# A logit copy on ScalarE, a reordered last block and later gathers in a fused attention-and-routing kernel

## The chip, the cores and the metric

The kernel runs on one core of one Trainium2 chip. The time is the device time of one execution in microseconds; where a run was repeated, the median is given. Everything else comes from a hardware profile of one execution, whose times are counted from the start of its span.

The engines of the core are PE (TensorE, matrix products; it takes transposes too), DVE (VectorE), ACT (ScalarE), POOL (GpSimd, which here also issues the gathers and scatters by row number) and SP (SyncE, which issues plain loads). Each runs its own list of instructions in order and waits on semaphores of the others. [...] DVE and ACT bring results from PSUM to SBUF.

## What is computed

Banded attention with a few global keys, then a mixture of experts in which each token goes to one expert:

```python
B, H, S, D = 4, 8, 768, 64            # n_global 8, n_local 96
scores = scale * q @ k.T  - slope[h] * dist     # only keys j < 8, or 0 <= i - j < 96
a   = exp(scores - max); a /= sum(a) + 1e-9
att = a @ v                            # (B, H, S, D), float32
x   = att.transpose(0, 2, 1, 3).reshape(B * S, H * D)     # 3072 tokens x 512

logits = x @ w_gate                    # 8 experts
e      = argmax(logits); gate = softmax(logits)[e]
out[t] = gate[t] * relu(x[t] @ w1[e]) @ w2[e]             # w1 512 x 1024, w2 1024 x 512
```

## The kernel before

The attention part goes over 24 blocks of 128 query tokens (4 sequences of 6 blocks). A block n needs its own 128 keys and the block before it, into whose first 32 rows the global keys and values of the sequence have been mixed. The blocks are software-pipelined: turn n of the loop computes the scores of block n, transposes q and k of block n+1, turns block n-2 into token rows, and multiplies the exponentials of block n-1 with their values.

```python
ps_s = tile_pool("ps_s", bufs=2, PSUM)     # scores, two banks each
ps_t = tile_pool("ps_t", bufs=3, PSUM)     # transposes, values, token rows
ps_r = tile_pool("ps_r", bufs=1, PSUM)     # row sums and logits: ONE buffer

def transposed(ps, dst, src, on, scale=1.0):
    pt = ps.tile([P, NPAIR, P], F32, tag="t", name="pt")
    for m in range(NPAIR):
        nc.tensor.transpose(pt[:, m, :], ..., ident[:])
    if on == "act":
        nc.scalar.activation(dst, pt[:], AF.Copy, bias=0.0, scale=scale)
    else:
        nc.vector.tensor_copy(out=dst, in_=pt[:])
# prep_q(n): transposed(..., "act", QS);  prep_k(n): transposed(..., "act" if n else "dve"),
# and POOL then makes ka, the keys of block n with the global keys in their first 32 columns

def mix_v(n):                              # global values into the block before
    if n % NBLK > 1:
        nc.gpsimd.tensor_copy(out=vts[n - 1][0:GW], in_=vts[n - n % NBLK][0:GW])

# scores(n): 16 to 32 matmuls into two sp tiles, DVE adds the bias: p <- sp, other
# exps(n, groups): ACT, p <- exp(p), one instruction of 128x1024 for each of two groups
# both(n): DVE, pb <- p[own keys] + p[keys before], two instructions of 128x512

def values(n):
    for m in range(NPAIR):                 # po tiles, two m in each
        ... nc.tensor.matmul(po[...], lhsT=vt[...], rhs=ps[n][...])
        if m % 2:
            nc.scalar.copy(ots[n][:, m - 1:m + 1], po[:, 0:2])
    pr = prs[n] = ps_r.tile([P, 4, P], F32, tag="r", name="pr")
    all_p = pbs.pop(n, None) or [p[:, :, :, 1, :] for p in ps[n]]
    ... nc.tensor.matmul(pr[..., 0, :], lhsT=one_in, rhs=all_p[...])      # row sums
    ... nc.tensor.matmul(pr[..., 0, :], lhsT=gate_w, rhs=ots[n][...])     # logits
    nc.scalar.copy(rs[:], pr[:, 0, :])
    return rs

def tokens(n, rs):
    nc.tensor.transpose(pr[:, 1, :], rs[:], ident[:])     # into the same pr bank
    ... nc.tensor.transpose(px[:, m, :], ot[:, m, :], ident[:])           # x4
    part = pr[:, 1, :].rearrange("p (m c) -> p m c", c=GW)
    nc.vector.tensor_scalar(den, part[...], 1e-9, None, ALU.add)
    nc.vector.reciprocal(rden, den)
    nc.vector.tensor_tensor(lh, part[...], rden, ALU.mult)
    nc.vector.tensor_reduce(lg[:, i, :], lh, AX.X, ALU.add)
    nc.vector.tensor_tensor(xr[...], px[...], rden, ALU.mult)
    # after the last block of a sequence: choose() = five small DVE instructions

for n in range(N + 1):                     # N = 24
    if n < N: scores(n)
    if n + 1 < N: prep_q(n + 1)
    ...
    if 0 < n <= N: both(n - 1)
    if n + 1 < N: prep_k(n + 1)
    if n < N and n != 1: exps(n, slice(0, 1 if n else 2))
    ...
    if n >= 2: tokens(n - 2, rs.pop(n - 2))            # and gates() for a whole sequence
    if n: rs[n - 1] = values(n - 1)
    if 0 < n < N: exps(n, slice(n != 1, 2))
    if n == N: ex.x_in_s(0, ps_t.tile(...))
    if n < N: mix_v(n)
    if i == 2 and b == B - 1:              # b, i = divmod(n - 2, 6): this is turn 22
        send()                             # two scatters of token rows to DRAM
        ex.early()
    ...                                    # dispatch() of a sequence: slots for its tokens
tokens(N - 1, rs.pop(N - 1))
```

`early` computes row numbers with eight small DVE instructions (the fifth gives `grow_s`), and has POOL gather two tiles of 128 finished token rows from DRAM (`xs <- xs_dram, grow_s`). `x_in_s` transposes such a tile on PE (`pt <- ident, xs`) and DVE copies it to SBUF (`xsT <- pt`). With it the first product of the experts begins (`up_s`, `u <- xsT, w`), about 163 us into the span; the experts fill the rest.

Of the kernel before, what the change touches and what calls it, by code (L numbers as in the profile page):

```python
# [9 lines left out]
F32 = mybir.dt.float32  # L10
BF16 = mybir.dt.bfloat16
I32 = mybir.dt.int32
AF = mybir.ActivationFunctionType
# [10 lines left out]
def kernel(  # L24
# [12 lines left out]
    nc = tc.nc  # L37

    P = 128
    B, H, S, D = q.shape  # L40
# [4 lines left out]
    NPAIR = H // 2  # L45
    NDC = DM // P
    NFC = F // P
    GW = 32
# [181 lines left out]
        nc.vector.tensor_tensor(x.rearrange("p (h d) -> p h d", d=D), po[:],  # L230
                                den[:].unsqueeze(2).to_broadcast([P, H, D]), ALU.mult)

    def transposed(ps, dst, src, on, scale=1.0):

        pt = ps.tile([P, NPAIR, P], F32, tag="t", name="pt")
        for m in range(NPAIR):
            nc.tensor.transpose(pt[:, m, :], src[:, 2 * m:2 * m + 2, :].rearrange("p a d -> p (a d)"),  # L237
                                ident[:])
        if on == "act":
            nc.scalar.activation(dst, pt[:], AF.Copy, bias=0.0, scale=scale)  # L240
        else:
            nc.vector.tensor_copy(out=dst, in_=pt[:])  # L242

    QS = 1.0 / float(D) ** 0.5

# [4 lines left out]
    def banded(stack, rt, pool, rows, ex, den_all):  # L250
# [29 lines left out]

        def prep_q(n):
            qts[n] = raw.tile([P, NPAIR, P], F32, tag="qt", bufs=2, name="qt")
            transposed(ps_t, qts[n][:], rawt[n]["q"], "act", QS)

        def prep_k(n):
            b, i = divmod(n, NBLK)
            kind = dict(tag="kt0") if i == 0 else dict(tag="kt", bufs=3)
            kts[n] = seq.tile([P, NPAIR, P], F32, name="kt", **kind)
            transposed(ps_t, kts[n][:], rawt[n]["k"], "act" if n else "dve")
            if i == 0:  # L290
                kas[n + 1] = kts[n][:]
            elif i + 1 < NBLK:
                t = raw.tile([P, NPAIR, P], F32, tag="ka", bufs=2, name="ka")
                nc.gpsimd.tensor_copy(out=t[:, :, GW:P], in_=kts[n][:, :, GW:P])  # L294
                nc.gpsimd.tensor_copy(out=t[:, :, 0:GW], in_=kts[n - i][:, :, 0:GW])
                kas[n + 1] = t[:]
# [78 lines left out]
        def exps(n, groups):  # L375
            for p in ps[n][groups]:
                z = p[:].rearrange("p a j t c -> p (a j) t c")
                z = z[:, :, 1, :] if n % NBLK == 0 else p[:].rearrange("p a j t c -> p (a j t c)")
                nc.scalar.activation(z, z, AF.Exp)  # L379
# [12 lines left out]
        def values(n):  # L392
            vals = [(t, vts[n - 1 + t]) for t in range(n % NBLK == 0, 2)]
            ots[n] = work.tile([P, NPAIR, P], F32, tag="ot", name="ot")
            for m in range(NPAIR):
                if m % 2 == 0:
                    po = ps_t.tile([P, NPAIR, P], F32, tag="t", name="po")
                for x, (t, vt) in enumerate(vals):
                    for a in range(2):
                        nc.tensor.matmul(po[D * a:D * a + D, m % 2, :], lhsT=vt[:, 2 * m + a, :],  # L400
                                         rhs=ps[n][m // 2][:, a, m % 2, t, :], start=(x == 0),
                                         stop=(x == len(vals) - 1), skip_group_check=True)
                if m % 2:
                    nc.scalar.copy(ots[n][:, m - 1:m + 1], po[:, 0:2])

            pr = prs[n] = ps_r.tile([P, 4, P], F32, tag="r", name="pr")
            all_p = pbs.pop(n, None) or [p[:, :, :, 1, :] for p in ps[n]]
            for a in range(2):
                for m in range(NPAIR):
                    nc.tensor.matmul(pr[GW * m:GW * m + GW, 0, :], lhsT=one_in[:, a, :],  # L410
                                     rhs=all_p[m // 2][:, a, m % 2, :], start=(a == 0),
                                     stop=False, skip_group_check=True)
            for m in range(NPAIR):
                nc.tensor.matmul(pr[GW * m:GW * m + GW, 0, :], lhsT=gate_w[:, m, :], rhs=ots[n][:, m, :],
                                 start=False, stop=True, skip_group_check=True)
            rs = work.tile([P, P], F32, tag="rs", name="rs")
            nc.scalar.copy(rs[:], pr[:, 0, :])
            del ps[n]
            return rs

        def tokens(n, rs):

            b, i = divmod(n, NBLK)
            pr, ot = prs.pop(n), ots.pop(n)
            nc.tensor.transpose(pr[:, 1, :], rs[:], ident[:])
            px = ps_t.tile([P, NPAIR, P], F32, tag="t", name="px")
            for m in range(NPAIR):
                nc.tensor.transpose(px[:, m, :], ot[:, m, :], ident[:])
            if i == 0:
                seqs[b] = new_rows(rows)  # L430
            xr, lg = seqs[b]
            part = pr[:, 1, :].rearrange("p (m c) -> p m c", c=GW)
            den, rden = den_all[:, 0, n, :], den_all[:, 1, n, :]
            nc.vector.tensor_scalar(den.rearrange("p (m a) -> p m a", a=2), part[:, :, 2 * E:2 * E + 2],
                                    1e-9, None, ALU.add)
            nc.vector.reciprocal(rden, den)
            shape = [P, NPAIR, 2, E]
            lh = work.tile(shape, F32, tag="lh", name="lh")
            nc.vector.tensor_tensor(lh[:], part[:, :, 0:2 * E].rearrange("p m (a e) -> p m a e", e=E),
                                    rden.rearrange("p (m a) -> p m a", a=2).unsqueeze(3)  # L440
                                    .to_broadcast(shape), ALU.mult)
            nc.vector.tensor_reduce(lg[:, i, :], lh[:].rearrange("p m a e -> p e (m a)"), AX.X, ALU.add)

            def x_rows():
                nc.vector.tensor_tensor(xr[:, i, 0:DM].rearrange("p (h d) -> p h d", d=D),
                                        px[:].rearrange("p m (a d) -> p (m a) d", d=D),
                                        rden.unsqueeze(2).to_broadcast([P, H, D]), ALU.mult)

            if n < N - 1:
                x_rows()  # L450
                if i == NBLK - 1:
                    seqs[b] += choose(pool, rt, xr, lg)
            else:
                seqs[b] += choose(pool, rt, xr, lg)
                x_rows()
# [9 lines left out]
        def send():  # L465
            for _ in range(min(2, len(sends))):
                sends.pop(0)()

        rs = {}
        for n in range(N + 1):  # L470
            if n < N:
                scores(n)
            if n + 1 < N:
                prep_q(n + 1)
            if n == 2:
                numbers = ex.clear_s()
            if n == 3:
                ex.numbers(*numbers)
            if n in (3, 4):
                biases(0, range(4 * n - 12, 4 * n - 8), "pool")  # L480
            if 0 < n <= N:
                both(n - 1)
            if n + 1 < N:
                prep_k(n + 1)
            if n < N and n != 1:
                exps(n, slice(0, 1 if n else 2))
            if n == 0:
                biases(1, (0, 1, 2, 3), "act")
            if n == 0:
                spare = ps_r.tile([P, 512], F32, tag="r", name="spare")  # L490
                for _ in range(4):
                    nc.tensor.matmul(spare[:], lhsT=idle[:, 0:P], rhs=idle[:], start=True, stop=True)
            if n + 3 < N:
                load(n + 3)
            for load_ in feed.pop(n, ()):
                load_()

            if n - 2 < N - NBLK + 2:
                send()
            b, i = divmod(n - 2, NBLK)  # L500
            if n >= 2:
                tokens(n - 2, rs.pop(n - 2))
                if i == 0 and b:
                    xr, _, oh, gates = seqs[b - 1]
                    gates()
            if n:
                rs[n - 1] = values(n - 1)
            if 0 < n < N:
                exps(n, slice(n != 1, 2))
            if n == N:  # L510
                ex.x_in_s(0, ps_t.tile([P, NPAIR, P], F32, tag="t", name="pt"))
            if n < N:
                mix_v(n)
            if i == 2 and b == B - 1:
                send()
                ex.early()
            if i == 0 and b > 0:
                sends += dispatch(pool, ps_t.tile([P, 512], F32, tag="t", name="pr"), rt, xr, oh)
                if b == B - 1:
                    send()  # L520
# [807 lines left out]
```

## Time and profile before

| what | value |
|---|---|
| time, median of 3 runs | 521.27 us (519.11 to 521.93) |
| span of the profiled execution | 514.3 us |
| 5 to 150 us (the blocks): PE busy | 140.7 us of 145 |
| the same: DVE, ACT, POOL busy | 115.9, 88.6, 51.7 us |
| 150 to 165 us (end of the blocks): PE busy | 12.2 us of 15, at a mean granted clock of 0.89 |
| 165 to 300 us (experts): PE busy | 134.5 us of 135 |
| 300 to 500 us (experts): PE busy | 199.2 us of 200 |

The rows by stretch are the sums of the view of busy time by window. "Busy" counts an engine's instructions; what an engine waits for is in the view of waits, where each line names the waiting instruction, the one that released it, the total in us, the number of times and the longest wait. In the timeline each line has the start and the length in us, the engine, the line of the kernel and the operation, with the number of instructions merged; a bracket at its end is the idle time before it and what ended that. The granted clock of PE is a share of full speed.

### The profile page before, as it was taken

What the parts mean: (1) busy time and instruction counts of PE and PEld (TensorE: products, weight loads), DVE (VectorE), ACT (ScalarE), POOL (GpSimd) and SP (SyncE); (2) the same over time, 40 slices, a digit from 0 to 9 for tenths busy, and PEclk for the clock granted to TensorE, in tenths of its full rate; (3) what the DMA queues carried; (4) which work ended last, traced back from release to release, by engine and by line L of the source; (5) the groups of instructions that cost most, each with busy time, mean ns of one, the idle gap of its engine ahead of it and who ended that gap; (6) DMA issues with size and microseconds to landing.
All of it is one profiled execution on the core that took longest, in us unless ns stands there. A gap on an engine that the chain in (4) does not pass through costs nothing.

```text
span 514.3 us, 12403 instructions
## 1 busy us (share of the span) xinstructions
PE 498.3 (97%) x5019; PEld 423.2 (82%) x5019; DVE 313.2 (61%) x665; ACT 159.4 (31%) x321; POOL 189.4 (37%) x285
## 2 busy tenths in 40 slices
PE   8999999999998999999999999999999999999995
PEld 5888888888887679679799688869969868896984
DVE  4777877977885747529588078128527705822741
ACT  4656666665652002112112012113102212211120
POOL 5531261251442574334373074034316305502503
PEclk9999999999998999999999999999999999999998
DMA  9998789799921331074191470047254108400101
GB/s 185 212 226 222 166 242 228 173 234 222 317 91 43 124 95 43 8 253 173 42 390 33 164 261 25 1 159 275 79 214 166 26 1 280 163 2 24 43 4 50
DMA packets 96333, 72.76 MB, mean 141 GB/s; under 512 B 79324, under 2 KB 79326, under 8 KB 96228
## 3 DMA queue, kind: packets, MB, share of 16 engines
q1 hardware_dynamic: 87808, 52.44, 37.4%
q0 software_dynamic: 7872, 19.01, 10.8%
q8 instruction: 54, 0.88, 0.7%
q14 instruction: 51, 0.42, 0.3%
q10 hardware_dynamic: 548, 0.02, 0.1%
HBM read 61.46 MB, written 14.73 MB: 148 GB/s over the span
## 4 chain that ended last, share of the span: by engine, by line
PE 82%; DVE 10%; issue 6%; POOL 1%; POOLq 0%; DVEq 0%
PE u L970 18%; PE u L798 10%; PE d L1032 9%; PE d L1041 7%; PE u L808 7%; PE sp L358 6%; PE po L400 5%; DVE p L372 4%; PE pt L237 3%; DVE pb L388 3%; PE d L808 3%; PE u L1139 3%; PE u L1114 3%; PE pr L410 2%; PE t L950 2%
## 5 line engine op out<-in xcount | busy, mean ns | idle before, releaser
L1048 DVE TENSOR_TENSOR UV<-UV,d 128x512 f32<-128x512 f32 x8 | 5.5, 688 | 110.9 <-ACT yu L1142 81.3
L732 POOL DMA_INDIRECT out_dram<-ys,to_u x8 | 8.3, 1039 | 142.6 <-ACT yu L1142 87.6
L372 DVE TENSOR_TENSOR p<-sp,other 128x1024 f32<-128x1024 f32 x40 | 47.1, 1219 | 21.4 <-PE sp L358 19.5
L798 PEld LDWEIGHTS u<-xsT,w 128*128 128x128 f32 x448 | 50.9, 192 | 2.2 <-DVE c L940 1.2
L798 PE MATMUL u<-xsT,w 128*128 128x128 f32 x448 | 51.8, 276 | 0.2 <-DVE xsT L790 0.2
L970 PE MATMUL u<-cx,c 128*128 128x128 f32 x384 | 48.1, 275 | 0.0
L379 ACT ACTIVATE p<-p 128x1024 f32<-128x1024 f32 (+1 forms) x48 | 47.3, 988 | 1.4 <-DVE p L372 1.1
L400 PE MATMUL po<-p,vt 128*64 128x128 f32 x704 | 45.1, 281 | 1.4 <-POOL vt L279 1.4
L970 PEld LDWEIGHTS u<-cx,c 128*128 128x128 f32 x384 | 45.5, 192 | 0.0
L400 PEld LDWEIGHTS po<-p,vt 128*64 128x64 f32 x704 | 39.3, 140 | 5.5 <-issue 2.7
L970 PE MATMUL u<-xT,w 128*128 128x128 f32 x256 | 39.5, 277 | 0.0
L358 PE MATMUL sp<-qt,kt 64*128 64x128 f32 x448 | 37.9, 275 | 0.9 <-DVE kt L242 0.9
L808 PE MATMUL u<-w,huT 128*128 128x512 f32 x80 | 35.1, 592 | 0.0
L970 PEld LDWEIGHTS u<-xT,w 128*128 128x128 f32 x256 | 34.2, 192 | 0.9 <-DVE cx L963 0.2
L358 PEld LDWEIGHTS sp<-qt,kt 64*128 64x128 f32 x448 | 31.0, 188 | 2.8 <-issue 2.3
L1032 PE MATMUL d<-c,ch 128*128 128x256 f32 x128 | 32.9, 379 | 0.0
L215 POOL DMA_INDIRECT xs_dram<-xr,slot_i x24 | 23.8, 993 | 17.9 <-DVE cnt L860 9.9
L294 POOL COPY ka<-kt 128x384 f32<-128x384 f32 x16 | 9.2, 576 | 56.2 <-ACT kt L240 56.2
L808 PEld LDWEIGHTS u<-w,huT 128*128 128x128 f32 x80 | 15.2, 190 | 17.0 <-issue 16.7
L388 DVE TENSOR_TENSOR pb<-p 128x512 f32<-128x512 f32 x40 | 27.9, 736 | 0.9 <-ACT p L379 0.9
L997 ACT COPY uv<-u 128x256 f32<-128x256 f32 x32 | 11.9, 373 | 51.2 <-PE u L970 51.1
L1032 PEld LDWEIGHTS d<-c,ch 128*128 128x128 f32 x128 | 24.3, 190 | 3.3
(255 smaller groups left out, 1030.5 us busy)
## 6 DMA issues: line engine op xcount, KB each, us to landing
w<-in_moe_w_dram SPq DMA_DIRECT2D x24, 1024.0 KB, 7.1
w<-in_moe_w_dram SPq DMA_DIRECT2D x16, 512.0 KB, 6.2
raw_q<-in_q_dram SPq DMA_DIRECT2D x24, 256.0 KB, 4.5
raw_k<-in_k_dram SPq DMA_DIRECT2D x24, 256.0 KB, 5.2
vt<-in_v_dram SPq DMA_DIRECT2D x24, 256.0 KB, 5.4
xs_dram<-xr,slot_i POOLq DMA_INDIRECT x24, 5.6
xg<-xs_dram,grow POOLq DMA_INDIRECT x16, 6.3
mu<-xs_dram,grow_e POOLq DMA_INDIRECT x16, 2.8
```

The source lines that it names most:

```text
L215: d = nc.gpsimd.indirect_dma_start(out=xs_dram[:], out_offset=bass.IndirectOffsetOnAxis(ap=slot_i[:, u:u + 1], axis=0), in_=xr[:, u, :].bi ...
L237: nc.tensor.transpose(pt[:, m, :], src[:, 2 * m:2 * m + 2, :].rearrange("p a d -> p (a d)"), ident[:])
L358: nc.tensor.matmul(sp[:, a, j, t, :], lhsT=kt[r, m, :], rhs=qts[n][r, m, :], start=True, stop=True, skip_group_check=True)
L372: nc.vector.tensor_tensor(z, sc, bi, ALU.add)
L379: nc.scalar.activation(z, z, AF.Exp)
L388: nc.vector.tensor_tensor(t[:].rearrange("p a j c -> p (a j) c"), z[:, :, 0, :], z[:, :, 1, :], ALU.add)
L400: nc.tensor.matmul(po[D * a:D * a + D, m % 2, :], lhsT=vt[:, 2 * m + a, :], rhs=ps[n][m // 2][:, a, m % 2, t, :], start=(x == 0), stop=(x ...
L798: nc.tensor.matmul(ph[:, i, :], lhsT=self.w[e % 2][0][:, c, ts(half * HF + i, P)], rhs=xT[:, c, :], start=(c == 0), stop=(c == NDC - 1), s ...
L808: nc.tensor.matmul(py[:].rearrange("p a b -> p (a b)"), lhsT=h[:, f, :], rhs=self.w[e % 2][1][:, f, :], start=(f == 0), stop=(f == NFC - 1 ...
L970: nc.tensor.matmul(bank[:, r, :], lhsT=lhs(k), rhs=rhs(k), start=first, stop=True, skip_group_check=True)
L1032: nc.tensor.matmul(self.half(i, j), lhsT=lhs, rhs=rhs, start=(f == 0 and j == 0), stop=True, skip_group_check=True)
L1041: nc.tensor.matmul(self.half(i, j), lhsT=lhs(f), rhs=rhs(f), start=False, stop=True, skip_group_check=True)
```

## The change

It has four parts. ScalarE copies the transposed logits and row sums of a block from the PSUM bank `pr` to SBUF, and VectorE reads the copy; the bank is then free for the next block after that copy and not after VectorE's reads. The gathers of the early rows are issued one turn later, behind the last mixing of values on POOL, so that they do not stand ahead of it in POOL's list. In the last turn the values of block 23 are computed ahead of the token rows of block 22, for which both exponentials of block 23 come together and its `pr` lies in a buffer of the scores pool. And the first transposed q and k are copied in halves, so that the first scores can start after half of each.

```diff
-    def transposed(ps, dst, src, on, scale=1.0):
+    def transposed(ps, dst, src, on, scale=1.0, parts=1):
...
-        if on == "act":
-            nc.scalar.activation(dst, pt[:], AF.Copy, bias=0.0, scale=scale)
-        else:
-            nc.vector.tensor_copy(out=dst, in_=pt[:])
+        for r in range(parts):
+            m = ts(r, NPAIR // parts)
+            if on == "act":
+                nc.scalar.activation(dst[:, m], pt[:, m], AF.Copy, bias=0.0, scale=scale)
+            else:
+                nc.vector.tensor_copy(out=dst[:, m], in_=pt[:, m])
... (prep_q and prep_k pass parts=1 if n else 2)
-            pr = prs[n] = ps_r.tile([P, 4, P], F32, tag="r", name="pr")
+            pr = prs[n] = (ps_r.tile([P, 4, P], F32, tag="r", name="pr") if n < N - 1 else
+                           ps_s.tile([P, 2, 2, 2, P], F32, tag="s", name="pr")[:, 0, 0])
... (tokens)
-            part = pr[:, 1, :].rearrange("p (m c) -> p m c", c=GW)
+            part = work.tile([P, P], F32, tag="part", name="part")
+            nc.scalar.copy(part[:], pr[:, 1, :])
+            part = part[:].rearrange("p (m c) -> p m c", c=GW)
... (loop)
-                exps(n, slice(0, 1 if n else 2))
+                exps(n, slice(0, 1 if 0 < n < N - 1 else 2))
...
+            if n == N:
+                rs[n - 1] = values(n - 1)
             if n >= 2:
                 tokens(n - 2, rs.pop(n - 2))
...
-            if n:
+            if 0 < n < N:
                 rs[n - 1] = values(n - 1)
-            if 0 < n < N:
+            if 0 < n < N - 1:
                 exps(n, slice(n != 1, 2))
...
             if i == 2 and b == B - 1:
                 send()
+            if i == 3 and b == B - 1:
                 ex.early()
```

More of the change, by code (lines that the diff above doesn't have):

```diff
@@ L282, in prep_q @@
             qts[n] = raw.tile([P, NPAIR, P], F32, tag="qt", bufs=2, name="qt")
-            transposed(ps_t, qts[n][:], rawt[n]["q"], "act", QS)
+            transposed(ps_t, qts[n][:], rawt[n]["q"], "act", QS, parts=1 if n else 2)
         def prep_k(n):
@@ L288, in prep_k @@
             kts[n] = seq.tile([P, NPAIR, P], F32, name="kt", **kind)
-            transposed(ps_t, kts[n][:], rawt[n]["k"], "act" if n else "dve")
+            transposed(ps_t, kts[n][:], rawt[n]["k"], "act" if n else "dve", parts=1 if n else 2)
             if i == 0:
```

## The prediction

> **What bounds the kernel now.** I read the page's busy shares first: PE has work for 97% of the span, so only its 16 us of idle, and any time at which its clock is lowered, can be won. The waits of PE say who holds it up:
>
> ```profile
> PE pr L410 <- DVE lh L439: 4.3, 9, 1.1
> PE po L400 <- POOL vt L279: 1.4, 1, 1.4
> PE sp L358 <- DVE kt L242: 0.9, 1, 0.9
> PE pr L425 <- ACT rs L417: 0.4, 1, 0.4
> PE u L798 <- DVE xsT L790: 0.2, 1, 0.2
> ```
>
> The change aims at the first three. Line 1 is the single `pr` bank: block n's row sums wait until VectorE has read block n-2's logits (`lh`). The timeline of PE places its nine waits: 21.5 us (0.27), 28.88 (1.06), 59.27 (0.27), 66.18 (0.33), 96.57 (0.27), 103.60 (0.45), 134.00 (0.27), 141.09 (0.52), 153.70 (0.83). The end of the blocks:
>
> ```profile
> 153.70 0.64 PE L410 MATMUL pr<-pb,one_in 128*32 128x128 f32 x16 [0.83 <-DVE lh L439]
> 155.00 0.33 PE L425 MATMUL pr<-ident,rs 128*128 128x128 f32 x1 [0.43 <-ACT rs L417]
> 157.15 3.31 PE L400 MATMUL po<-p,vt 128*64 128x128 f32 x32 [1.39 <-POOL vt L279]
> 161.27 0.66 PE L789 MATMUL pt<-ident,xs 128*128 128x128 f32 x4
> 162.71 0.49 PE L798 MATMUL u<-xsT,w 128*128 128x128 f32 x2 [0.18 <-DVE xsT L790]
> ```
>
> The values of block 23 (third line) take 3.31 us; in every full block before it the same 32 records take 1.97. The windows show why (after the stretch: length, busy time and count of PE, PEld, DVE, ACT, POOL, then the clock):
>
> ```profile
> 157.00:159.00 2.00, 1.85 (x18) 1.86 (x20) 1.06 (x3) 0.00 (x0) 1.00 (x2) 0.50 0.27 103
> 159.00:160.00 1.00, 1.00 (x14) 1.00 (x12) 0.00 (x0) 0.37 (x1) 0.00 (x0) 0.53 0.00 0
> ```
>
> With 0.76 in 156 to 157, PE ran at half clock from about 156.5 to 159.9, 3.4 us, of which 2.8 after 157.15: that cost 1.4 us beside the waits. On POOL two gathers (from 153.24 and 154.60) stood ahead of the mixing at 155.94, though its input had been free since the values of block 22 ended at 152.87.
>
> [...] the issues list has 3.7 us to landing for these two gathers, so a gather issued later is not free.
>
> **Part 1, the copy on ScalarE.** It adds 23 executed copies of 128x128; the like copy `rs` takes 0.27 us, with the next instruction 0.16 after its start. ScalarE has room (88.6 us busy of 145). What counts is the place in its list: after the first exponential of the turn, ahead of the two `ot` copies. VectorE's `den` now waits for it. In most turns that costs VectorE 0.3 us, which it has. Not in the turns that begin a sequence (7, 13, 19):
>
> ```profile
> 51.02 0.59 ACT L240 ACTIVATE kt<-pt 128x512 f32<-128x512 f32 x1
> 51.49 1.06 ACT L379 ACTIVATE p<-p 128x1024 f32<-128x1024 f32 x1
> 52.44 0.65 ACT L404 COPY ot<-po 128x256 f32<-128x256 f32 x2
> ```
>
> Here `den` started at 51.27. The copy can start at 52.44 and end at 52.71, so `den` starts at 52.77, 1.5 us late, and with it the choice of experts, which ended at 53.90 and now ends at 55.4. VectorE had 0.80 us of idle before its next large addition:
>
> ```profile
> 54.69 2.35 DVE L372 TENSOR_TENSOR p<-sp,other 128x1024 f32<-128x1024 f32 x2 [0.80 <-PE sp L358]
> 61.60 2.35 DVE L372 TENSOR_TENSOR p<-sp,other 128x1024 f32<-128x1024 f32 x2
> 63.87 1.59 DVE L388 TENSOR_TENSOR pb<-p 128x512 f32<-128x512 f32 x2
> ```
>
> The addition thus starts at 55.4, 0.7 late, and from there VectorE has no idle until 66.9; the chain that ended last runs through it there. The `pb` of block 7 ends at 58.56 + 0.72 = 59.28, that of block 8 at 65.46 + 0.72 = 66.18. PE no longer waits for `lh` (66.03) but still needs `pb`: it starts at 66.2 to 66.3, where it started at 66.18. The wait is exchanged, not removed. So the six waits at 59, 66, 97, 104, 134 and 141 us (2.1 us) give nearly nothing: 0.3 in all[...]. The `ot` copies of these three turns come 0.16 us later, which the same wait swallows.
>
> The two early waits do go. At 21.50 `pb` is ready at 20.78 and PE free at 21.19: 0.31 earlier, less 0.07 because row sums without a wait take that much longer to hand over (35.15 to 36.01 against 21.50 to 22.29), so 0.24. At 28.88 VectorE is held by extra work of that turn; `pb` ends at 28.16, PE starts at 28.27: 0.61. Part 1: 0.24 + 0.61 + 0.3 = 1.15 us.
>
> **Part 2, halves.** First scores start when half of `kt` is there, about 0.3 us earlier than 7.71. But VectorE's bias chain, which ends at 9.67, sets block 0's additions, and the scores of block 1 (10.79) need the first of those (about 10.6). I count 0.07.
>
> **Parts 3 and 4, the end of the blocks,** in times of the trace before. Both exponentials of block 23 now run ahead of the logit copy: 150.6 to 152.76, the copy to 152.93, so the row sums of block 22 start at 153.0, not 153.70, and end at 153.9. POOL mixes from 152.95 to 153.6 (0.60, as in other blocks). Values of block 23: 153.9 to 155.87 at full clock. VectorE then holds PE: `den` to `xr` of block 21 (1.55 us) from 153.0 to 154.5, `early` (1.42, from its place at 148.04 to 149.46) to 155.87, and only then the two `pb` of block 23, to 157.15. PE waits some 1.2 us, ends row sums at 157.95 and the transposes of block 22 at 158.6. The gathers wait for `grow_s` (155.3), start at 155.6 and land 3.3 later (in the raw records the first started at 153.24 and landed at 156.55): 158.9. PE transposes `xs` at 159.0; VectorE, after `xr` of block 22 (to 160.1), copies `xsT` to 160.75. First product of the experts at 160.8, where it was 162.71: 1.9 us, of which 1.4 is the lost half clock. After that nothing changes: PE is busy for 134.5 of 135 us from 165, and each engine's list is the same.
>
> Sum against the profile: 1.15 + 0.07 + 1.9 = 3.1 us, if PE keeps full clock.
>
> **Will it?** Between 155.87 and 160.8 PE has only 0.86 us of row sums, transposes and 2.2 us of idle: a low stretch of 4.9 us, where the one before (152.87 to 157.15) had 4.3. [...] A dip in the new place would fall on dense matmuls and cost up to 1.7 us. The timed runs of before may mostly have had no dip; then the end gives 0.5 us only and the sum is 1.7. Weighing no dip on either side, one before only and one after only (1.7, 3.1, near 0.2), I take 2.1: 521.27 - 2.1 = 519.2.
>
> **Rivals.** (a) All nine waits for `lh` vanish and the end runs smoothly: 4.3 + 1.4 + 1.4 + 0.4 = 7.5 us, 513.8. Against it is VectorE's unbroken run from 54.69 to 66.9. (b) The logit copy makes VectorE the bound at every sequence change and PE loses there, 0.3 us in each of three, while the gathers land late: no gain, 521 to 522. For it: at 51.27 `den` was ready 1.2 us before ScalarE can copy. (c) The gathers become the wait: were landing 5.6 us, as for the scatters in the issues list, PE would stand until 161.3 and the end would give nothing but the lost clock. The 3.3 of the same gathers speaks against it.
>
> **Range and chances.** Three runs of before spread over 2.8 us, which is as much as the gain; the sum itself runs from 0.2 (dip after only) to some 5. So 516.5 to 521.5. A gain of 2% is 10.4 us, more than all PE waits named above; a loss of 2% would need a new wait of 0.4 us in every block. Within 2%: 0.97.
>
> **What would show it.** Right: waits of PE for `lh` gone, and in their place waits for `pb` at the second and third blocks of sequences 2 to 4; VectorE's idle between turns 7 and 9 gone; `den` after the ScalarE copy at about 52.8; the gathers starting 2 us later than before; about 1 us of PE wait for `pb` ahead of the last row sums; first product of the experts some 3 us earlier than 162.71. Wrong: if the waits near 59 and 66 us vanish without a successor, part 1 is worth 2 us more; if the clock dips again between 156 and 163, the end is worth 1.5 us less; if PE waits for the gathers by more than 0.5 us, part 3 has turned into a new wait.

## The result, and the profile after

Before takes 521.16 us (median of six), after 517.15 us (median of six): a ratio of 0.993, with a 95% interval of 0.9907 to 0.9952. The change is 4.0 us faster, less than 1%. The prediction was 519.2 us, a gain of 2.1, with 516.5 to 521.5 as its range.

The profiles say something else. The profile of before is of an execution of 516.22 us, shorter than every timed run of before (519.11 to 521.93). The profile of after is of one of 517.69 us, like its timed runs (516.20 to 517.69). Laid side by side, the two profiles show after as the slower one. The waits of PE in the profile of after (us in total, times, longest):

```profile
PE pr L413 <- ACT part L436: 2.7, 4, 1.7
...
PE pr L413 <- DVE pb L390: 1.1, 3, 0.5
PE u L806 <- DVE gates L801: 0.9, 1, 0.9
...
PE pt L797 <- DMA xs<-xs_dram,grow_s: 0.7, 1, 0.7
PE sp L360 <- DVE kt L244: 0.6, 1, 0.6
```

All waits for `lh` are gone, and so is the one for the mixed values. In their place stand waits for the new copy (`part`), for the sums `pb`, for the gathers and for VectorE ahead of the experts. The timeline of PE at the end of the blocks:

```profile
155.84 0.72 PE L413 MATMUL pr<-pb,one_in 128*32 128x128 f32 x14 [1.68 <-ACT part L436]
...
156.82 1.97 PE L402 MATMUL po<-p,vt 128*64 128x128 f32 x32
159.26 0.41 PE L413 MATMUL pr<-pb,one_in 128*32 128x128 f32 x4 [0.47 <-DVE pb L390]
...
162.06 0.63 PE L797 MATMUL pt<-ident,xs 128*128 128x128 f32 x4 [0.65 <-DMA xs<-xs_dram,grow_s]
...
164.15 3.81 PE L806 MATMUL u<-xsT,w 128*128 128x128 f32 x32 [0.91 <-DVE gates L801]
```

The values of block 23 take 1.97 us, at full clock (they took 3.31), but the first product of the experts starts at 164.15, where before had 162.71. The stretches that showed the half clock before (length, busy time and count of PE, PEld, DVE, ACT, POOL, then the clock):

```profile
157.00:159.00 2.00, 1.79 (x32) 1.54 (x30) 1.90 (x10) 0.74 (x3) 0.53 (x1) 1.00 0.00 0
159.00:160.00 1.00, 0.55 (x9) 0.28 (x13) 0.81 (x2) 0.21 (x1) 0.70 (x2) 1.00 0.00 0
```

And the turn that begins the second sequence, on ScalarE and VectorE, as the prediction looked at it:

```profile
50.76 1.06 ACT L381 ACTIVATE p<-p 128x1024 f32<-128x1024 f32 x1
51.71 0.27 ACT L436 COPY part<-pr 128x128 f32<-128x128 f32 x1
...
52.01 0.17 DVE L439 TENSOR_SCALAR den_all<-part 128x8 f32<-128x8 f32 x1 [1.40 <-ACT part L436]
...
54.56 2.35 DVE L374 TENSOR_TENSOR p<-sp,other 128x1024 f32<-128x1024 f32 x2
```

So two questions were open: what the timed runs of before do that its profile does not show, and which part of the change is worth what.

### The profile page after: what moved, and what is told of

Read it like the earlier page. It is cut to its first block, busy times and chain, and to the rows that moved or that the text cites. A ratio compares the mean times of both kernels' runs of the same rounds, so it can differ in the third digit from the quotient of the medians.

```text
span 515.9 us, 12427 instructions
## 1 busy us (share of the span) xinstructions
PE 498.8 (97%) x5019; PEld 422.2 (82%) x5019; DVE 316.8 (61%) x666; ACT 162.3 (31%) x346; POOL 190.5 (37%) x285
## 4 chain that ended last, share of the span: by engine, by line
PE 86%; issue 5%; DVE 5%; DMA 1%; SPq 1%; POOL 1%; ACT 1%; POOLq 0%; ACTq 0%
PE u L978 18%; PE u L806 10%; PE d L1040 9%; PE sp L360 8%; PE d L1049 7%; PE u L816 7%; PE po L402 6%; PE pt L237 4%; PE d L816 3%; PE pr L413 3%; PE u L1147 3%; PE u L1122 3%; DVE p L374 2%; PE t L958 2%; PE px L431 1%
## 5 line engine op out<-in xcount | busy, mean ns | idle before, releaser
L402 PE MATMUL po<-p,vt 128*64 128x128 f32 x704 | 43.7, 276 | 0.8 <-issue 0.5
L402 PEld LDWEIGHTS po<-p,vt 128*64 128x64 f32 x704 | 38.1, 137 | 5.0 <-issue 3.9
```

## The experiments

Four chips took part, and the times on them differ. I name them by the time of the kernel before: A 515.6 us, B 522.4, C 520.9, D 516.2. Each was used in one session only, so what is said here of a chip may belong to the session instead; no run separates the two. Which chip the first comparison ran on is not recorded; by its times it is like B and C, while the first profile of before looks like A and D. Ratios are to runs of before on the same chip; 95% intervals in brackets.

**Before, unchanged (chip A).** No edit.

> The kernel before, unchanged, for a second profile and for the clock of each run. The profiled execution of before took 516.2 us, its timed runs 519.1 to 521.9; after takes 516.2 to 517.7 in both. Theory A, the clock: the timed runs of before lose some 4 us to stretches at half clock that the first profile had only once; then their spans are 517 to 520 at granted clocks of 0.98 to 0.99, and a profile of such a run shows two or more stretches of 3.4 us at half clock. Theory B, a wait: the clock is 0.994 or more in the long runs too, and a second profile shows 3 to 5 us more of waits than the first.

Measured: 515.07 us, ratio 0.9998 [0.9982, 1.0014]. None of these 14 executions came near 521, so the first comparison was not reproduced on this chip, and the 521 was not tested. The clock was: of the 62 runs of before here, 25 have a granted clock of 0.995 or less, and they are 1.6 us longer on average than the others (516.6 against 515.1 in one group, 516.3 against 514.6 in the other); one more execution, of 523.32 us at a clock of 0.947, is left out. I take the 1.6 us as the price of one dip (a stretch at half clock), in 40% of the executions: 0.65 us of the mean. The profile here is of an execution without a dip, and its end serves as the base for chip A:

```profile
157.04 1.97 PE L400 MATMUL po<-p,vt 128*64 128x128 f32 x32 [1.39 <-POOL vt L279]
...
161.27 3.84 PE L798 MATMUL u<-xsT,w 128*128 128x128 f32 x32 [0.18 <-DVE xsT L790]
```

**The copy alone (chip A).**

```diff
-            part = pr[:, 1, :].rearrange(...)
+            part = work.tile([P, P], F32, tag="part", name="part")
+            nc.scalar.copy(part[:], pr[:, 1, :])
+            part = part[:].rearrange(...)
```

> Before with the ScalarE copy of the logits alone. By the working of the prediction (two early waits go, six are exchanged for waits on pb): 1.15 us less than before, some 520.0. Rival a, all nine waits for lh vanish: 4.3 us less, 516.9. Rival b, the copy makes VectorE the bound at each change of sequence: 521 to 522. If the gain of the whole change is the clock at the end of the blocks: 521 as before, within 0.5.

Measured: 513.68 us, ratio 0.9971 [0.9955, 0.9988], a gain of 1.5 us (0.6 to 2.3), with the expected 1.15 inside it. Neither rival fits. Three lines of PE's timeline show the exchange:

```profile
51.86 0.64 PE L410 MATMUL pr<-p,one_in 128*32 128x128 f32 x16 [0.33 <-ACT part L433]
...
140.30 0.52 PE L410 MATMUL pr<-pb,one_in 128*32 128x128 f32 x10 [0.40 <-DVE pb L388]
...
159.76 3.84 PE L800 MATMUL u<-xsT,w 128*128 128x128 f32 x32 [0.18 <-DVE xsT L792]
```

The first recurs at 89.13 and 126.45: at each new sequence PE now waits 0.33 us for the copy. The experts start at 159.76, against 161.27.

**The end of the blocks alone (chip A).** After without the copy and without the halves.

> Before with the end of the blocks alone (values of block 23 ahead of the tokens, both exponentials of block 23 together, row sums of block 23 in another bank, gathers behind the last mix of values), without the ScalarE copy and without halves. By the prediction 1.9 us less where the old place dips to half clock, 0.5 where it does not: 519.3 to 520.7. If the whole gain of 4 us is the clock at this place: 517.2, with granted clocks of 0.997 as in after. If it is the copy: 521.

Measured: 514.82 us, ratio 0.9986 [0.9974, 0.9998]. The values of block 23 start 2.64 us earlier than before (154.40 against 157.04), and the experts at 161.24 against 161.27:

```profile
154.40 1.97 PE L402 MATMUL po<-p,vt 128*64 128x128 f32 x32
...
159.04 0.63 PE L795 MATMUL pt<-ident,xs 128*128 128x128 f32 x4 [0.74 <-DMA xs<-xs_dram,grow_s]
...
161.24 5.44 PE L804 MATMUL u<-xsT,w 128*128 128x128 f32 x32 [1.03 <-DVE lh L442]
```

All of the 2.64 us is lost again: 0.74 in front of the gathered rows, 1.03 in front of the first product, which waits for VectorE, and the rest largely in the transposes of block 22, which now stand behind these values (157.54 to 158.30). What is left in the time, 0.8 us, fits the dips: one run of 14 has the low clock, against 25 of 62. The profile happens to be of that one run, and it shows the dip where the prediction feared it, in the first products of the experts: half clock from about 161.5 to 164.9, and 5.44 us where 32 such products take 3.81 at full clock.

**After without halves (chip A).** `parts=1` throughout.

> After without the first copies in halves. By the prediction 0.07 us longer than after: 517.2. Since the trace of after shows the second transposes waiting 1.1 us for their load, I expect no difference at all, within 0.3. A rival: the halves start the whole chain 0.3 to 1.0 us earlier: 517.5 to 518.2.

Measured: 514.37 us, ratio 0.9976 [0.9966, 0.9987]; on this chip the expected 517 of the first comparison means nothing, and the ratio counts. By the medians it is 0.7 us slower than the copy alone; the intervals overlap, but the profiles agree: the experts start at 160.97, not at 159.76. None of its 22 runs has the low clock. The end of the blocks:

```profile
152.59 0.64 PE L413 MATMUL pr<-pb,one_in 128*32 128x128 f32 x16 [0.28 <-ACT part L436]
...
153.48 1.97 PE L402 MATMUL po<-p,vt 128*64 128x128 f32 x32
156.22 0.41 PE L413 MATMUL pr<-pb,one_in 128*32 128x128 f32 x4 [0.77 <-DVE pb L390]
...
159.03 0.63 PE L797 MATMUL pt<-ident,xs 128*128 128x128 f32 x4 [0.66 <-DMA xs<-xs_dram,grow_s]
...
160.97 3.81 PE L806 MATMUL u<-xsT,w 128*128 128x128 f32 x32 [0.76 <-DVE gates L801]
```

**After, unchanged (chip B).** No edit.

> After, unchanged, beside before on the same chip. The first comparison gave 4.0 us less than before, but with before at 521 in its timed runs and 516 in its profile. Theory A (what the traces of the parts add up to: without halves 1.2 us less than before): 1.0 to 1.6 us less, and the additions of scores, which start up to 1.4 us late in the first profile of after, start in time here (first product of the experts near 161.0, not 164.15). Theory B: the 4 us of the first comparison are the change's own and come back, ratio near 0.993.

Measured: 517.72 us, ratio 0.9917 [0.9897, 0.9937]. Theory A fell: the first product of the experts is at 164.13, as in the first profile of after, and the gain of 4 us is back. So it was no chance of one comparison: where before takes 521 to 522, after gains 4 us; where before takes 515.6, all but the halves gains 1.2 (after itself was not run there).

**Copy, and the gathers moved (chip B).**

```diff
                 send()
+            if i == 3 and b == B - 1:
                 ex.early()
```

> The ScalarE copy and, of the end of the blocks, only the gathers behind the last mix of values (the order of values and tokens as before). With the copy alone 513.7, and there the values of block 23 wait 0.68 us for the mix. Theory A: that wait goes, but the index arithmetic now stands 1.4 us ahead of the sums pb of block 23 on VectorE and the gathers land near 158.6: the first product of the experts moves by -0.2 to +0.5 us, 513.5 to 514.2. Theory B (the prediction's): the earlier values carry through to the experts, 0.7 us less, 513.0.

Measured: 517.48 us, ratio 0.9918 [0.9896, 0.9940]. The wait for the mix is gone. The copy alone was not run on B; by the ratios (0.9912 for it on C, below) nothing is gained over it, as theory A has it, whose absolute numbers were for chip A.

**Copy, and the order of the last turn (chip B).** `values(23)` ahead of `tokens(22)`, both exponentials together, the other bank; the gathers as before.

> The ScalarE copy and, of the end of the blocks, only the order (values of block 23 ahead of the tokens of block 22, both exponentials together, the other bank), gathers as before ahead of the mix. Theory A: the mix holds the values as before, and the tokens of block 22 now come behind them, so that the copy xsT, which stands behind their VectorE work, ends about 1.2 us later: 514.9. Theory B: the order is what brings the gain of the end: 513.0 or less.

Measured: 517.74 us, ratio 0.9921 [0.9901, 0.9941]. No gain over the copy alone here either, by the same ratio. After, this one and the one above can't be told apart by their times; in their profiles the experts start at 164.13, 163.08 and 162.80.

**Three things moved in after (chip B, then chip D).**

```diff
-            if n < N and n != 1:
-                exps(n, slice(0, 1 if 0 < n < N - 1 else 2))
...
             if n == N:
+                ex.early_rest()            # lim, inv_s, loc, row
                 rs[n - 1] = values(n - 1)
+                ex.x_in_s(0, ...)          # was behind the tokens of block 22
             if n >= 2:
                 tokens(n - 2, rs.pop(n - 2))
+            if 1 < n < N:
+                exps(n, slice(0, 1 if n < N - 1 else 2))
...
             if i == 2 and b == B - 1:
                 send()
+                ex.early()                 # indices only
             if i == 3 and b == B - 1:
-                ex.early()
+                ex.early_gathers()
```

> After with three things moved: the copy of the logits ahead of the turn's exponential on ScalarE, the indices of the two gathers computed a turn earlier than the gathers (which stay behind the last mix of values), and the transposes and copy of the gathered rows ahead of the tokens of block 22. Theory A (the end of after is held by VectorE's order and by gathers that wait for their indices; the turns at each new sequence by the place of the copy): waits of PE for part and pb go at turns 7, 13, 19 (1.0 us), and the first product of the experts comes 1.5 to 3 us earlier than in after: 511 to 512.5. Theory B (VectorE's sum of work or the clock is the limit): no better than the copy alone, 513.7.

Measured on B: 514.43 us, ratio 0.9854 [0.9833, 0.9875], 3.3 us less than after beside it (517.72); the intervals of the two ratios do not touch. The 511 to 512.5 of theory A was for the times of chip A.

> The kernel with three things moved, again, beside before. Where before takes 521 to 522: 513.5 to 514.5 (ratio 0.985 again). Where before takes 515.6: 511.5 to 512.5, since without late signals only what the traces of the early chips show can be won, 1.0 us at the new sequences and 1.5 us or more at the end over after (514.4).

Measured on D: 511.00 us, ratio 0.9911 [0.9886, 0.9935]. That is 5.2 us less than before on D, and 0.5 below the 511.5 to 512.5 that was expected. It beats before on both kinds of chip, and after on B, the only place where the two ran side by side. On D nothing waits for `part` or `pb` any more, and the end reads:

```profile
151.84 1.97 PE L402 MATMUL po<-p,vt 128*64 128x128 f32 x32
...
155.34 0.66 PE L804 MATMUL pt<-ident,xs 128*128 128x128 f32 x4 [0.66 <-DMA xs<-xs_dram,grow_s]
...
157.01 3.84 PE L813 MATMUL u<-xsT,w 128*128 128x128 f32 x32
```

**Before again (chip C).** No edit.

> The kernel before again, for a profile on a chip where it takes 521 to 522 us. So far its two profiles (514.3 and 513.4 us of span) are of executions of 515 to 516 us, while after, where it takes 517.5, shows signals of PE that reach ScalarE and VectorE some 1 us late in the turns with scatters (9 to 11, 15 to 17, 20 to 23). Theory A: before has the same late signals and pays more for them, because its logits are read by VectorE from the one bank: a profile of a 521 us execution shows 5 to 7 us more of PE waits than the first one, in these turns, with the experts' part as long as before. Theory B: the difference lies behind 165 us, in the experts. If this execution takes 515 again, neither is tested.

Measured: 521.26 us, ratio 1.0006 [0.9989, 1.0023], and the profile is of an execution of 522.16 us. Theory A holds. First the waits of PE:

```profile
PE pr L410 <- DVE lh L439: 8.4, 12, 2.0
PE pr L425 <- ACT rs L417: 1.3, 1, 1.3
...
PE po L400 <- ACT qt L240: 1.1, 1, 1.1
```

The nine waits of 4.3 us have become twelve of 8.4. Where they come from is seen in turn 10, in the timelines of PE, ScalarE, VectorE and POOL:

```profile
73.46 0.43 PE L414 MATMUL pr<-ot,gate_w 128*32 128x128 f32 x8
```

```profile
75.43 0.27 ACT L417 COPY rs<-pr 128x128 f32<-128x128 f32 x1 [2.54 <-PE sp L358]
```

```profile
76.22 2.36 DVE L372 TENSOR_TENSOR p<-sp,other 128x1024 f32<-128x1024 f32 x2 [2.44 <-PE sp L358]
```

```profile
73.32 0.99 POOL L215 DMA_INDIRECT xs_dram<-xr,slot_i  x1 [0.17 <-issue]
74.62 0.97 POOL L215 DMA_INDIRECT xs_dram<-xr,slot_i  x1 [0.31 <-issue]
```

The products that `rs` waits for end at 73.89, and ScalarE, idle, starts the copy at 75.43: 1.54 us later. (The bracket names the scores of block 11, because the profile goes by the time of the signal; `rs` does not read them.) The raw trace puts the delay into the signal: the event of PE's semaphore that lets the copy go is at 75.36, 0.07 us before the copy. PE itself runs on meanwhile, with the scores from 73.82. In the profile on chip A it is 0.10 us in the same block, with the event at 73.28:

```profile
73.35 0.27 ACT L417 COPY rs<-pr 128x128 f32<-128x128 f32 x1 [0.57 <-PE pr L414]
```

Block 14 of the first profile of after has the delay in the same place: the event comes 0.79 us after PE's last record, and the copy 0.08 us after the event. The measure of the delay for all 24 blocks (start of `rs` less the end of PE's last record for it):

| profile | chip | late blocks (us) | all others |
|---|---|---|---|
| before, first comparison | not recorded | none | 0.05 to 0.11 |
| after, first comparison | not recorded | 14 (0.86), 20 (0.81), 21 (1.09), 23 (0.66) | 0.05 to 0.10 |
| before | A | none | 0.05 to 0.12 |
| copy alone | A | 22 (0.38) | 0.05 to 0.10 |
| before | C | 8 (0.94), 9 (1.54), 14 (1.57), 15 (1.03), 20 (1.55), 21 (1.62), 22 (0.99) | 0.05 to 0.12 |
| after | B | 14 (0.89), 20 (0.86), 21 (1.11), 23 (0.69) | 0.04 to 0.11 |
| copy alone | C | 14 (1.05), 20 (0.82), 21 (1.11), 22 (0.86) | 0.04 to 0.11 |
| copy and gathers | B | 14 (1.10), 20 (1.54), 21 (1.13), 22 (0.38) | 0.05 to 0.10 |
| copy and order | B | 14 (1.12), 20 (1.53), 21 (1.11) | 0.05 to 0.15 |
| three moved | B | 8 (0.86), 14 (1.66), 20 (1.56), 21 (1.13), 22 (0.32) | 0.05 to 0.11 |
| three moved | D | none | 0.04 to 0.11 |

All late blocks lie in turns in which POOL issues scatters or gathers. The same kernel, with scatters at the same places, has none on A. The two entries of 0.38 for block 22 are of another kind: there PE's event came in time, 0.03 us after the last record. The profile of after in the first comparison has late blocks like those on B, and that of before has none: the two were taken on different chips or in different sessions.

**The copy alone again (chip C).**

> The ScalarE copy alone again, beside before. Where before takes 521 to 522, theory A (the copy takes VectorE's reads of the one bank out of the chain of late signals): 517 to 518, the whole gain of after; theory C (the 4 us come from the end of the blocks): 520. Where before takes 515.6: 513.7 as in the first comparison.

Measured: 516.11 us, ratio 0.9912 [0.9879, 0.9946]: the gain of after on B (0.9917), from the copy alone. Theory C fell. The 8.4 us of waits for `lh` are gone, and much less has taken their place:

```profile
PE pr L425 <- ACT rs L417: 1.2, 1, 1.2
PE pr L410 <- ACT ot L404: 1.2, 1, 1.2
...
PE pr L410 <- ACT part L433: 1.0, 3, 0.3
...
PE pr L410 <- DVE pb L388: 0.4, 1, 0.4
```

The three things moved come out below this too: 0.9854 on B, and 0.9911 on D against 0.9971 for the copy alone on A, with intervals that do not touch.

**Before, with the scatters of two sequences moved (chip D).**

```diff
-            if n - 2 < N - NBLK + 2:
+            if n in (12, 18):
+                for _ in range(3):
+                    send()
+            elif 20 <= n < N - NBLK + 4:
                 send()
```

> Before, with the scatters of the first two sequences moved: all six in turn 12 and all six in turn 18, where before has two in each of turns 9 to 11 and 15 to 17. Theory A, that the scatters bring the late signals of PE (where before takes 521): the copies rs and the additions p of turns 9 to 11 and 15 to 17 come in time, block 12 starts within 0.3 us of 88.5 and no longer 1.8 us or more after it, and late signals appear in turns 12, 13, 18 and 19 in their place; 519 to 521 in all. Rival, the late signals belong to those turns for another reason (loads of weights, the second part of a sequence): they stay in turns 9 to 11. Where before takes 515.6 there are no late signals and nothing is told apart: 515 to 516.5.

Measured: 517.55 us, ratio 1.0035 [1.0012, 1.0057]. Chip D has before's short times (516.2), and this profile has no late block, so it tells nothing of their cause; six scatters in one turn cost 1.3 us there (0.6 to 2.9). That the scatters bring the late signals stays a guess from their place.

## Why the prediction was right or wrong

One table answers most points. It cuts the time up to the first product of the experts in three: up to the values of block 3, from there to those of block 22, and the end (all in us, from the timelines of PE).

| kernel | chip | to block 3 | 3 to 22 | end | experts at |
|---|---|---|---|---|---|
| before | A | 33.09 | 117.70 | 10.48 | 161.27 |
| copy alone | A | 32.32 | 117.77 | 9.67 | 159.76 |
| end alone | A | 33.11 | 117.69 | 10.44 | 161.24 |
| after without halves | A | 32.59 | 117.76 | 10.62 | 160.97 |
| three moved | D | 32.06 | 116.81 | 8.14 | 157.01 |
| before | C | 33.22 | 122.66 | 12.72 | 168.60 |
| copy alone | C | 32.28 | 118.99 | 10.58 | 161.85 |
| after | B | 32.13 | 119.99 | 12.01 | 164.13 |
| three moved | B | 32.14 | 119.07 | 9.22 | 160.43 |

**The base: wrong.** The prediction subtracted a sum of waits from 521.27 that were all read from a profile of 516.22. It even guessed that the timed runs "may mostly have had no dip", which would make them shorter than the profile, not 3 to 5 us longer. The difference was there to be seen. As far as chip C stands for the first comparison, it is the late signals: before on C has its experts at 168.60, 7.3 us after A, of which 1.4 is a dip (the values of block 23 take 3.41 us) and 5.9 are waits. With the copy it is 161.85 against 159.76, 2.1. So the copy saves 3.8 us of lateness there, partly because fewer blocks are late (four, not seven; five with three things moved). Why fewer are, no run tells. That is a gain that no step of the prediction has. That 517.15 lies in the stated range is therefore luck: the range was wide, and the gain of 4.0 us is of other terms than those summed.

**Part 1, the two early waits (0.24 and 0.61): right.** 0.77 us at block 3, 0.91 with the 0.14 by which the first block started later in that run.

**Part 1, six waits "exchanged, not removed" (0.3 in all): right in kind, off in size.** From block 3 to 22 the copy gives -0.07 us. VectorE's `den` started at 52.01 in after; 52.77 was predicted, in a block that began 0.73 later. Its large addition started at 54.56, predicted 55.4. Rival (a) is refuted by this. But PE pays first at another place than named: at the row sums of the sequence's first block, which wait for the copy behind the exponential (0.33, three times). For `pb` it waits at the third blocks only. Block 20 has 0.40 in the view of waits; at blocks 8 and 14 the row sums begin with the first `pb` and halt for the second (in block 8 it ends at 65.20, and they go on at 65.25), which the view counts as busy: with the logits they take 1.29 and 1.34 us there, and 0.95 in most blocks. The 0.3 was my estimate, for shorter reads by VectorE, and they were not there: on chip A `den` takes 157 ns at the least from SBUF (median 206, in after without halves) and 157 (median, in before) from PSUM, `lh` 224 (median) from both.

**Part 2, halves (0.07): none seen.** The values of block 0 start at 13.63 to 13.99 us in the profiles of after and at 13.67 to 14.10 without halves. PE waits 0.6 us for its first scores, not 0.9, and then 0.9 to 1.1 us for the second block's load.

**Parts 3 and 4 in themselves: right in order, 0.7 us short in size.** The prediction's times are on the clock of the trace before, where the values of block 22 start at 150.90. In after without halves, on chip A, they start at 150.35, so 0.55 us is added here:

| step | predicted | measured | with 0.55 added | late by |
|---|---|---|---|---|
| row sums of block 22 | 153.0 | 152.59 | 153.14 | 0.14 |
| values of block 23 | 153.9 | 153.48 | 154.03 | 0.13 |
| first gather issued | 155.6 | 155.43 | 155.98 | 0.38 |
| transposes of gathered rows | 159.0 | 159.03 | 159.58 | 0.58 |
| first product of the experts | 160.8 | 160.97 | 161.52 | 0.72 |

The lateness grows in two places: VectorE takes 1.86 us from `den` to `xr` of block 21 (152.57 to 154.43), not 1.55, ahead of the index arithmetic, and the gathered rows reach PE 3.6 us after their gather, not 3.4. PE's wait for `pb` was 0.77 and 0.19, predicted 1.2; its wait for the gathers 0.66, where the prediction said that over 0.5 would be a new wait. It is one, and rival (c) is right in part.

**Parts 3 and 4 as a gain (1.9, or 0.5 without the dip): wrong.** Two steps failed. The size is one: the first product at 161.52 is no earlier than in the trace before without its dip (162.71 less 1.34 is 161.37), and the end alone gives 0.04 us (10.48 to 10.44). The comparison is the other: the 0.83 us of `lh` at 153.70 was counted here, but the copy alone removes it (end 10.48 to 9.67). Against the copy alone the two parts make the end 0.95 us longer, and the time 0.7 us: the index arithmetic stands ahead of `pb`, the gathers are issued 2.9 us later than with the copy alone (155.43 against 152.50), and `xsT` comes behind VectorE's work for block 22. The run with three things moved shows it from the other side: indices a turn ahead of their gathers and `xsT` ahead of the tokens make the end 8.14, 2.5 us less; which of the two gives how much was not run. Its middle, 116.81, is 0.95 less than that of after without halves; I put this down to the copy's new place ahead of the exponential, which was not run by itself, and the two middles are from different chips.

**The dip: place and cost right, chances the wrong way round.** That the longer low stretch (4.9 us against 4.3) is the likelier to dip was my estimate. In the old order of before the low clock stands in 25 of 62 runs on A, 7 of 11 on B, 14 of 28 on C and 12 of 18 on D. With the new end of the blocks it stands in one of 48: none of 22 of after without halves, one of 14 of the end alone, and none of six of after in the first comparison and six on B. The stretch that I feared, from the end of the values of block 23 to the experts, had PE busy for 3.13 of 5.36 us (158.79 to 164.15) in the first profile of after, which kept full clock, and for 3.06 of 4.87 in that of the end alone, where the half clock followed and cost 1.6 us. In the profile of before the dip began within such a stretch too, with 1.63 of 4.28 us busy (152.87 to 157.15). What decides whether the clock drops, these runs do not show. Fewer dips are worth some 0.65 us to the change on A.

Of rival (b), the copy indeed cost 0.33 us at each of three new sequences, but "no gain" it was not.

## What to carry to other kernels

Before working on a profile, lay its own time beside the timed runs: if it is outside their spread, the profile lacks something that the time contains. A part of a change is worth what it adds to the other parts, not to the kernel before; the same 0.8 us of wait can be removed only once. Try the copy that frees a buffer ahead of the long instruction in its engine's list, and when a gather moves back leave its index arithmetic where it was: the fastest run here does both, though neither was run by itself.

## What was not expected of the hardware

In the sessions on two of four chips PE's signals come late in a few turns, all with scatters or gathers issued in them: ScalarE's copy `rs` starts 0.3 to 1.7 us after PE's last record of what it waits for. In all other turns it is 0.04 to 0.15 us, and on the other two chips too, but for one 0.38. This costs the kernel before about 1% (on C 5.9 us of waits ahead of the experts, by comparison with A). In turn 10 PE's own list runs on in that time, so the delay is found only as waits of the other engines, and of PE for them later. The cause is open, and so is whether it is of the chip or of the session.
